# A decode kernel: a second copy of x loaded in 18 one-row pieces on GpSimd's queue and in row groups of 1, 2, 4 and 8 on ScalarE's

## The chip, the cores and the metric

The kernel runs on one core of a Trainium2 chip. The metric is the device time in microseconds of one execution. Each set of runs gives a median; one execution is also recorded by the hardware profiler, and the profile's times count from the start of that execution's span.

## The reference

One decode step: x of 8 rows and 512 columns is normalised, goes through attention over the last 2048 positions of a key and value cache (32 query heads, 8 cache heads of 128), and through a gated unit whose result gates the attention's output.

```python
B, Sq, D = 8, 1, 512                  # Hq, Hkv, Sk, Dh = 32, 8, 8192, 128; F = 1792
xn = layernorm(x)
q = (xn @ wq)                         # to [B, 32, 1, 128]
k = k_cache[:, :, Sk - W:, :]         # W = 2048, each cache head for 4 query heads
v = v_cache[:, :, Sk - W:, :]
p = softmax(q @ k^T * Dh ** -0.5)
s = (p @ v) @ wo
g = silu((sigmoid(xn @ w_gate) * (xn @ w_up)) @ w_down)
out = x + s * g
```

Inputs and output are bf16. The change concerns the x of the last line.

## The kernel before

**Data.** wq, the windows of both caches, the three weights of the gated unit and wo are read once, 81 MB. They go through `ring`, nine tiles of up to 2048 KB, and all their loads are issued by SyncE (`load`, L88). The order is the list `loads` (L138 to L146): two halves of wq, then tiles of k (`k_sb`) and v (`v_sb`) in the order in which they are due, with w_gate, w_up (`wg_sb`, `wu_sb`) and w_down (`wd_sb`) before the end and wo (`wo_sb`, in pieces) last. In SyncE's order the first are wq0, wq1, k0, k1, k2, k3, v0, k4, v1, then k5, v2, k6, v3, k7, v4, k8. `issue_loads` (L164) issues the next ones whose place in the ring was released.

**Order.** The program's order is written by hand (`manual_schedule`): each engine runs its instructions in the order of the source. The loop at L610 goes through slots t. One slot turns a quarter of a k tile on DVE (`k_turn`, L422), multiplies it with q on the PE (`qk`, L435), and, for an earlier batch row, runs the softmax (`soft_max_part`, `soft_exp`, `soft_turn`, `soft_spread`, `soft_mask`) and the product with v (`pv`, L549; ScalarE copies it out at L560). A batch row has SPB = 8 slots. ScalarE's copy `pc_bf` (L495) belongs to `soft_spread`.

**x.** x is loaded twice. `x_bf` (L97, ScalarE's queue) is for the normalisation. `x2_sb` (L181, called x_sb in the profile) is for the sum at the end: 64 partitions, of which 0 to 7 hold columns 0 to 255 of the 8 rows and 32 to 39 hold columns 256 to 511. It is set to zero on GpSimd and then filled by two loads from GpSimd's queue (L184), ahead of all else that GpSimd does: `ident`, the zeros of `qz_sb` (L194), `SumM` (L232 to L254) and `ones` (L264).

**The end.** After the last tile of v, the PE multiplies with w_down and wo (`a_ps`, L662, piece by piece as wo lands); DVE computes `prod` (L673) and `y_bf` (L675), which reads x2_sb; SyncE and ScalarE each issue one half of the output (L677). Then SyncE checks the semaphores of all engines and queues, two at a time, before the engines meet for the last time (L706 in the profile).

**Semaphores of the loads.** The loads of SyncE and ScalarE take turns on eight completion semaphores, HW0 to HW7, those of GpSimd on eight others, SW0 to SW7. A load that takes a semaphore waits, on its issuing engine, until the load that had it before has landed. Before the change, x_bf has HW0, wq0 has HW1, wq1 HW2, k0 to k3 have HW3 to HW6, v0 HW7, k4 HW0, v1 HW1: so v1 waits for wq0, k5 for wq1, v2 for k0.

Of the kernel before, what the change touches and what calls it, by code (L numbers as in the profile page):

```python
# [10 lines left out]
def kernel(  # L11
# [13 lines left out]
    nc = tc.nc  # L25
    P = 128
    B, _, D = A_x.shape
# [23 lines left out]
    SPB = NG * NJ  # L51
# [10 lines left out]
    NCOL = 2  # L62
    DC = D // NCOL
# [29 lines left out]
    def ring_tile(shape, name):  # L93
        return ring.tile(shape, bf16, name=name, tag="ring", align_bytes=ALIGN)
# [7 lines left out]
    for kh in range(2):  # L102
        t = ring_tile([P, KH, Hq * Dh], f"wq_sb{kh}")
# [76 lines left out]
    issue_loads()  # L180
    x2_sb = work.tile([NCOL * 32, DC], bf16, name="x2_sb")  # L181
    nc.gpsimd.memset(x2_sb[:], 0.0)
    for j in range(NCOL):
        nc.gpsimd.dma_start(  # L184
            out=x2_sb[32 * j : 32 * j + B, :],
            in_=A_x.flatten_outer_dims()[:, DC * j : DC * (j + 1)],
        )

    ident = consts.tile([P, P], bf16, name="ident")
    make_identity(nc, ident[:])  # L190
# [18 lines left out]
        out=rstd[:], in_=mv[:, 1:2], func=AF.Sqrt, bias=eps_t[:], scale=1.0  # L209
# [4 lines left out]
        out=xn_bf[:],  # L214
# [7 lines left out]
    for kt in range(KT):  # L222
        nc.tensor.transpose(
            out=xnT_ps[:, kt, :], in_=xn_bf[:B, kt::KT], identity=ident[:B, :B]
# [8 lines left out]
    for off in range(-rep * (NQ - 1), rep * NQ, rep):  # L233
        nc.gpsimd.affine_select(
            out=SumM[:],
            in_=SumM[:],
# [9 lines left out]
        out=SumM_blk,  # L246
        in_=SumM_blk,
# [7 lines left out]
        out=SumM_blk,  # L255
        in_=SumM_blk,
# [5 lines left out]
    )  # L262
    ones = consts.tile([P, P], f32, name="ones")
    nc.gpsimd.memset(ones[:], 1.0)  # L264

    Jneg = consts.tile([P, NQ], f32, name="Jneg")
    nc.vector.tensor_reduce(
        out=Jneg[:],
        in_=ident[:].rearrange("p (a j r) -> p j a r", j=NQ, r=rep),
# [4 lines left out]
        out=Jneg[:], in0=Jneg[:], scalar1=-scale, scalar2=None, op0=ALU.mult  # L274
# [4 lines left out]
        out=Hm[:],  # L279
        in_=ident[:].rearrange("p (a gl) -> p gl a", gl=GL),  # L280
# [5 lines left out]
    for w in (32, 64):  # L286
        Sel[w] = consts.tile([P, w], f32, name=f"Sel{w}")
        nc.vector.tensor_reduce(
            out=Sel[w][:],
            in_=ident[:].rearrange("p (a m) -> p m a", m=w),  # L290
# [7 lines left out]
    for Q in range(NQ):  # L298
        nc.vector.tensor_copy(
            out=spread[:, :, Q, 32 * Q : 32 * (Q + 1)].rearrange(  # L300
                "m c (k g) -> m c g k", g=GL
            ),
            in_=ident[:].rearrange("m (g c k) -> m c g k", c=C4, k=KQ),
# [74 lines left out]
    def q_out(gg, q_ps, on_dve):  # L378
        HW = rep * Dh
        q_sb = ppool.tile([P, HW], bf16, name="q_sb", tag="p_bf")  # L380
        nc.scalar.copy(
            out=q_sb[:].rearrange("p (y e w) -> p y e w", e=2, w=32),
            in_=q_ps[:].rearrange("p (y w e) -> p y e w", e=2, w=32),
        )
        qT_sb = ppool.tile([P, HW], bf16, name="qT_sb", tag="pt_bf")
        nc.vector.transpose(out=qT_sb[:], in_=q_sb[:])  # L386
        for gl in range(GL):
            for Q in range(NQ):
                c0 = rep * NQ * gg + rep * Q
                out = qz_sb[32 * Q : 32 * (Q + 1), :, GL * gg + gl, :, c0 : c0 + rep]  # L390
                in_ = qT_sb[32 * gl : 32 * (gl + 1), :].rearrange(
                    "p (r y b) -> p b y r", r=rep, b=32
                )[:, :B]
                if Q in on_dve:
                    nc.vector.tensor_copy(out=out, in_=in_)  # L395
                else:
                    nc.scalar.copy(out=out, in_=in_)  # L397
# [16 lines left out]
    def k_turn(t):  # L414

        i, j = divmod(t, NJ)
        kw = (
            k_tiles[i][:, CC * j : CC * (j + 1), :]
            .rearrange("p c d -> p (c d)")
            .bitcast(f32)  # L420
        )
        nc.vector.transpose(out=kw, in_=kw)  # L422

    def qk(t):

        i, j = divmod(t, NJ)
        b, gg = divmod(i, NG)
        a, e = divmod(j, 2)
        if gg == 0 and j == 0:
            s_tiles[b] = psum.tile([P, CH * KQ], f32, name="s_ps")  # L430
        kT = k_tiles[i][:].rearrange(
            "p c (a k g e) -> p c a k g e", a=NA, k=KQ, e=2
        )
        for gl in range(GL):
            nc.tensor.matmul(  # L435
                s_tiles[b][32 * gl : 32 * (gl + 1), :],
                lhsT=qz_sb[:, b, GL * gg + gl, j, :],
                rhs=kT[:, :, a, :, gl, e],
                start=(gg == 0 and j == 0),
                stop=(gg == NG - 1 and j == NJ - 1),  # L440
                tile_position=(0, 32 * gl),
                skip_group_check=True,
            )

    def soft_max_part(b):
        mx = small.tile([P, 1], f32, name="mx")
        nc.vector.reduce_max(out=mx[:], in_=s_tiles[b][:], axis=AX.X)  # L447
        mj = small.tile([P, NQ], f32, name="mj")
        nc.vector.tensor_scalar(  # L449
            out=mj[:], in0=Jneg[:], scalar1=mx[:], scalar2=None, op0=ALU.mult  # L450
        )
        return mj

    def soft_exp(b, mj):
        mb_ps = psum1.tile([P, NQ], f32, name="mb_ps", tag="misc")
        nc.tensor.matmul(mb_ps[:], lhsT=SumM[:], rhs=mj[:], start=True, stop=True)  # L456
        nm = small.tile([P, 1], f32, name="nm")
        nc.vector.tensor_reduce(out=nm[:], in_=mb_ps[:], axis=AX.X, op=ALU.min)  # L458
        den128 = small.tile([P, 1], f32, name="den128")
        p_bf = ppool.tile([P, CH * KQ], bf16, name="p_bf")  # L460
        nc.scalar.activation(  # L461
            out=p_bf[:],
            in_=s_tiles.pop(b)[:],
            func=AF.Exp,
            bias=nm[:],
            scale=scale,
            accum_out=den128[:],
        )
        e_tiles[b] = (p_bf, den128)

    def soft_turn(b):

        p_bf = e_tiles[b][0]
        pt_bf = ppool.tile([P, CB, NG, NQ, rep], bf16, name="pt_bf")
        nc.vector.transpose(  # L475
            out=pt_bf[:].rearrange("p c g q r -> p (c g q r)"), in_=p_bf[:]
        )
        pt_tiles[b] = pt_bf
# [22 lines left out]
    def soft_mask(b):  # L501

        pc = pc_tiles.pop(b)[:].rearrange("p y (h n) -> p (y h) n", h=2)
        pT_tiles[b] = ppool.tile([P, CB * NG * 2, GL, 2 * rep], bf16, name="pT_sb")
        for gl in range(GL):
            nc.vector.tensor_scalar(  # L506
                out=pT_tiles[b][:, :, gl, :],
                in0=pc,
                scalar1=Hm[:, gl : gl + 1],
                scalar2=None,  # L510
                op0=ALU.mult,
            )

    def soft_den_part(b):
        den128 = e_tiles.pop(b)[1]
        dh = small.tile([P, Hq], f32, name="dh")
        nc.vector.tensor_scalar(
            out=dh[:].rearrange("p (G g r) -> p G g r", G=NG, g=GL),
            in0=SumM[:].rearrange("p (g G j r) -> p j G g r", g=GL, G=NG, j=NQ)[:, 0],
            scalar1=den128[:],  # L520
            scalar2=None,
            op0=ALU.mult,
        )
        return dh
# [85 lines left out]
    for t in range(NSLOT + PV_LAG):  # L610
        u = t - PV_LAG
        b, ph = (t - QK_LAG) // SPB - 1, (t - QK_LAG) % SPB
        in_b = 0 <= b < B
        if in_b and ph == 3:
            soft_mask(b)
            dh_of[b] = soft_den_part(b)
        if t < NSLOT:
            k_turn(t)
        if t == 1:
            q_out(1, q_tiles[1], (0,))  # L620
        if in_b and ph == 2:
            soft_turn(b)
        if QK_LAG <= t < NSLOT + QK_LAG:
            qk(t - QK_LAG)
        if in_b and ph == 0:
            mj_of[b] = soft_max_part(b)
        if in_b and ph == 1:
            soft_exp(b, mj_of.pop(b))
        if u >= NJ and u % NJ == 0:
            pv_sum(u // NJ - 1)  # L630
        if u >= 0:
            pv(u)
        if in_b and ph == 2:
            soft_spread(b)
        if in_b and ph == 4:
            soft_den(b, dh_of.pop(b))
        if t % NJ == NJ - 1 and QK_LAG <= t < NSLOT + QK_LAG:
            released.add((0, t // NJ - 1))
        if u >= 0 and u % NJ == NJ - 1:
            released.add((1, u // NJ))  # L640
        issue_loads()
        if u == NSLOT - 2 * NJ - 1:
            unit_in(wg_sb[0])
            unit_in(wu_sb[0])
            released |= {(2, 0), (2, 1)}
            issue_loads()
        if u == NSLOT - 2 * NJ:
            unit_mid()
        if u == NSLOT - NJ:
            o_rows(0)  # L650
# [25 lines left out]
    for c in range(NCOL):  # L676
        queues[c].dma_start(  # L677
            out=out.flatten_outer_dims()[:, DC * c : DC * (c + 1)],
            in_=y_bf[32 * c : 32 * c + B, :],
# [31 lines left out]
```

## Time and profile before

| | |
|---|---|
| median of 3 runs | 198.26 us (198.17 to 198.59) |
| the profiled execution | 198.21 us |
| its span | 196.5 us |
| PE busy | 138.2 us (70%) |
| DVE busy | 117.0 us (60%) |
| ScalarE busy | 32.6 us (17%) |
| GpSimd busy | 9.3 us (5%) |
| read from HBM | 81.02 MB, 412 GB/s over the span |

The profile gives stretches of the span with each engine's busy time and number of instructions, the granted PE clock, the busy share of the 16 DMA engines and what they moved:

```profile
0.00:13.00 13.00, 2.19 (x20) 0.96 (x21) 7.18 (x18) 1.58 (x2) 9.35 (x21) 1.00 0.86 345
13.00:43.00 30.00, 15.84 (x82) 3.94 (x81) 23.98 (x36) 12.08 (x26) 0.00 (x0) 0.93 1.01 433
43.00:100.00 57.00, 51.41 (x303) 17.64 (x300) 38.24 (x63) 7.62 (x15) 0.00 (x0) 0.89 1.01 430
...
183.00:193.00 10.00, 8.14 (x94) 6.49 (x92) 1.14 (x2) 0.38 (x1) 0.00 (x0) 0.71 0.91 363
193.00:196.50 3.50, 0.28 (x2) 0.09 (x1) 0.69 (x2) 0.00 (x0) 0.00 (x0) 0.87 0.02 5
```

The columns are the stretch in us, its length, then PE, PE weight load, DVE, ScalarE (ACT) and GpSimd (POOL). GpSimd works in the first stretch alone. Beside these views, the trace has a record of each DMA packet (queue, start, time taken, size) and of each of the 16 completions of a load, one by each DMA engine; it doesn't name the engine. In the profile a name followed by q, as SPq, is an engine's instruction queue.

### The profile page before, as it was taken

The numbers are of one execution on the slowest core, as the hardware profiler recorded it, in microseconds if no ns is written. First come the engines' busy times: TensorE is split into PE (matmuls) and PEld (weight loads), VectorE is DVE, ScalarE is ACT, GpSimd is POOL, SyncE is SP. The second block draws the span as 40 slices with busy tenths as digits, with TensorE's granted clock in tenths as the row PEclk, the third lists the DMA queues.
The fourth block names the chain that finished last, engine by engine and source line by source line (L and its number), as shares of the span: only waits on it lengthen the run. The fifth ranks groups of instructions, "written<-read, shape, count | busy, mean of one in ns | idle before, by whom it ended". The sixth has DMA issues, their size and how long they took to land.

```text
span 196.5 us, 2699 instructions
## 1 busy us (share of the span) xinstructions
PE 138.2 (70%) x1112; PEld 57.6 (29%) x1112; DVE 117.0 (60%) x200; ACT 32.6 (17%) x68; POOL 9.3 (5%) x21
## 2 busy tenths in 40 slices
PE   0340078669998987899789278946794779674783
PEld 0110011032324222423333044404240424443661
DVE  3818999746686828664777277837773750361101
ACT  3008540410121102101210021002100210340000
POOL 8820000000000000000000000000000000000000
PEclk9999999955999997879999957996888587996579
DMA  6999999999999999999999999999999999999991
GB/s 215 429 427 427 430 434 429 440 434 427 434 427 434 427 427 427 430 434 430 430 434 434 424 427 440 430 425 427 430 434 430 427 431 434 423 424 420 411 391 41
DMA packets 6860, 81.19 MB, mean 413 GB/s; under 512 B 792, under 2 KB 1088, under 8 KB 2112
## 3 DMA queue, kind: packets, MB, share of 16 engines
q1 hardware_dynamic: 6752, 81.01, 97.1%
q8 instruction: 8, 0.13, 0.2%
q10 hardware_dynamic: 32, 0.01, 0.1%
q14 instruction: 4, 0.03, 0.0%
q0 software_dynamic: 64, 0.01, 0.0%
HBM read 81.02 MB, written 0.01 MB: 412 GB/s over the span
## 4 chain that ended last, share of the span: by engine, by line
DMA 72%; DVE 17%; PE 8%; ACT 1%; issue 1%; SPq 0%; DVEq 0%; ACTq 0%
DMA k_sb<-in_A_k_cache_dram 47%; DMA wd_sb<-in_B_w_down_dram 14%; DVE k_sb L422 11%; DMA wq_sb<-in_A_wq_dram 6%; DMA wo_sb<-in_A_wo_dram 5%; PE pT_ps L486 3%; PE s_ps L435 3%; DVE qz_sb L395 2%; PE acc_ps L549 1%; DVE mx L447 1%; DVE qT_sb L386 1%; DVE pt_bf L475 1%; ACT L461 1%; PE q_ps L367 1%; PE mb_ps L456 0%
## 5 line engine op out<-in xcount | busy, mean ns | idle before, releaser
L422 DVE STREAM_TRANSPOSE k_sb<-k_sb 128x1024 f32<-128x1024 f32 x64 | 75.9, 1219 | 16.6 <-DMA k_sb<-in_A_k_cache_dram 16.5
L435 PE MATMUL s_ps<-k_sb,qz_sb 128*32 128x512 bf16 x256 | 68.7, 1065 | 16.4 <-DVE k_sb L422 11.6
L549 PE MATMUL acc_ps<-v_sb,pT_sb 128*32 128x256 bf16 (+1 forms) x416 | 35.3, 345 | 3.9 <-DMA v_sb<-in_A_v_cache_dram 2.6
L549 PEld LDWEIGHTS <-pT_sb 128*32 128x32 bf16 (+1 forms) x416 | 12.5, 109 | 33.2 <-issue 27.0
L506 DVE TENSOR_SCALAR pT_sb<-pc_bf,Hm 128x512 bf16<-128x512 bf16 x32 | 9.1, 349 | 18.3 <-ACT pc_bf L495 18.3
L435 PEld LDWEIGHTS <-qz_sb 128*32 128x32 bf16 x256 | 8.3, 100 | 34.0 <-issue 26.1
L560 ACT COPY acc_sb<-acc_ps 128x256 f32<-128x256 f32 (+1 forms) x16 | 7.2, 453 | 63.2 <-PE acc_ps L549 63.2
L486 PE MATMUL pT_ps<-pt_bf,spread 128*128 128x128 bf16 x128 | 12.5, 272 | 6.3 <-DVE pt_bf L475 6.3
L570 PEld LDWEIGHTS oT_ps<-Sel,acc_sb 128*128 128x128 f32 x88 | 11.8, 202 | 14.3 <-ACT acc_sb L560 8.5
L570 PE MATMUL oT_ps<-Sel,acc_sb 128*128 128x16 f32 x88 | 13.4, 276 | 1.1 <-ACT acc_sb L560 1.1
L486 PEld LDWEIGHTS <-spread 128*128 128x128 bf16 x128 | 10.8, 123 | 10.8 <-DVE pt_bf L475 10.8
L456 PE MATMUL mb_ps<-mj,SumM 128*128 128x4 f32 x16 | 3.5, 286 | 14.3 <-DVE mj L449 14.3
L461 ACT ACTIVATE p_bf<-s_ps,nm 128x512 bf16<-128x512 f32 x8 | 5.5, 687 | 46.5 <-DVE nm L458 46.5
L577 DVE TENSOR_TENSOR oT_sb<-oT_ps,rden 128x16 bf16<-128x16 f32 x16 | 2.6, 160 | 11.7 <-PE oT_ps L570 11.7
L456 PEld LDWEIGHTS mb_ps<-mj,SumM 128*128 128x128 f32 x16 | 2.8, 218 | 22.5 <-DVE mj L449 20.6
L397 ACT COPY qz_sb<-qT_sb 32x128 bf16<-32x128 bf16 x20 | 8.3, 413 | 3.0 <-DVE qT_sb L386 2.7
L530 DVE RECIPROCAL rden<-den_ps 128x32 f32<-128x32 f32 x8 | 2.8, 351 | 7.3 <-PE den_ps L528 7.3
L495 ACT CAST pc_bf<-pT_ps 128x512 bf16<-128x512 f32 x8 | 4.7, 587 | 13.1 <-PE pT_ps L486 13.1
L367 PE MATMUL q_ps<-wq_sb,xnT_sb 128*32 128x512 bf16 x32 | 3.8, 625 | 4.0 <-DMA wq_sb<-in_A_wq_dram 4.0
L475 DVE STREAM_TRANSPOSE pt_bf<-p_bf 128x512 bf16<-128x512 bf16 x8 | 5.4, 679 | 1.9 <-ACT p_bf L461 1.9
L662 PE MATMUL a_ps<-wo_sb,o_sb 128*32 128x256 bf16 x64 | 5.5, 315 | 1.0 <-DMA wo_sb<-in_A_wo_dram 0.9
L447 DVE TENSOR_REDUCE mx<-s_ps 128x1 f32<-128x512 f32 x8 | 5.3, 657 | 0.0
(61 smaller groups left out, 61.9 us busy)
## 6 DMA issues: line engine op xcount, KB each, us to landing
k_sb<-in_A_k_cache_dram SPq DMA_DIRECT2D x16, 2048.0 KB, 31.8
v_sb<-in_A_v_cache_dram SPq DMA_DIRECT2D x16, 2048.0 KB, 29.5
wq_sb<-in_A_wq_dram SPq DMA_DIRECT2D x2, 2048.0 KB, 9.7
wo_sb<-in_A_wo_dram SPq DMA_DIRECT2D x2, 1024.0 KB
wg_sb<-in_B_w_gate_dram SPq DMA_DIRECT2D x1, 1792.0 KB, 29.3
wu_sb<-in_B_w_up_dram SPq DMA_DIRECT2D x1, 1792.0 KB, 30.1
wd_sb<-in_B_w_down_dram SPq DMA_DIRECT2D x1, 1792.0 KB, 27.6
wo_sb<-in_A_wo_dram SPq DMA_DIRECT2D x3, 512.0 KB, 23.5
```

The costliest lines, as they stand in the source:

```text
L397: nc.scalar.copy(out=out, in_=in_)
L422: nc.vector.transpose(out=kw, in_=kw)
L435: nc.tensor.matmul(s_tiles[b][32 * gl : 32 * (gl + 1), :], lhsT=qz_sb[:, b, GL * gg + gl, j, :], rhs=kT[:, :, a, :, gl, e], start=(gg == 0 ...
L447: nc.vector.reduce_max(out=mx[:], in_=s_tiles[b][:], axis=AX.X)
L456: nc.tensor.matmul(mb_ps[:], lhsT=SumM[:], rhs=mj[:], start=True, stop=True)
L461: nc.scalar.activation(out=p_bf[:], in_=s_tiles.pop(b)[:], func=AF.Exp, bias=nm[:], scale=scale, accum_out=den128[:],)
L475: nc.vector.transpose(out=pt_bf[:].rearrange("p c g q r -> p (c g q r)"), in_=p_bf[:])
L486: nc.tensor.matmul(pT_ps[:, :, c4, :], lhsT=spread[:, c4, Q, :], rhs=pt[:, :, Q, :], start=(Q == 0), stop=(Q == NQ - 1), skip_group_check= ...
L506: nc.vector.tensor_scalar(out=pT_tiles[b][:, :, gl, :], in0=pc, scalar1=Hm[:, gl : gl + 1], scalar2=None, op0=ALU.mult,)
L549: nc.tensor.matmul(acc_tiles[i][w * c : w * (c + 1), :], lhsT=pT[:, 32 * y : 32 * y + w], rhs=v_tiles[i][:, ch : ch + n_ch, :].rearrange(" ...
L560: nc.scalar.copy(out=acc_sb[:], in_=acc_tiles.pop(i)[:])
L570: nc.tensor.matmul(oT_ps[:], lhsT=acc_sb[:, Dh * c : Dh * (c + 1)], rhs=sel[:, c // 2, c % 2], start=(c == 0), stop=(c == n_ch - 1),)
```

## The change

The two loads of x2_sb are replaced by 23 smaller ones.

- Rows 0 to 7 of the left half (partitions 0 to 7) are loaded one row at a time, row 0 in four pieces and each other row in two: 18 loads of 31, 37, 79, 109, 17, 239, 23, 233, 29, 227, 59, 197, 83, 173, 89, 167, 107 and 149 columns. They are on GpSimd's queue, after `ones`.
- The right half (partitions 32 to 39) is loaded on ScalarE's queue in five loads: the first 17 columns in groups of 1, 2, 4 and 1 rows, and the other 239 columns of all 8 rows. They stand in the loop at slot t = 16, which on ScalarE is after the first `pc_bf` copy and before the first `acc_sb` copy.

```diff
-    for j in range(NCOL):
-        nc.gpsimd.dma_start(
-            out=x2_sb[32 * j : 32 * j + B, :],
-            in_=A_x.flatten_outer_dims()[:, DC * j : DC * (j + 1)],
-        )
+    x_rows = A_x.flatten_outer_dims()
+    CUT = ((31, 68, 147), (17,), (23,), (29,), (59,), (83,), (89,), (107,))
+
+    def load_x2_top():
+        for b in range(B):
+            cuts = (0, *CUT[b], DC)
+            for c0, c1 in zip(cuts, cuts[1:]):
+                nc.gpsimd.dma_start(
+                    out=x2_sb[b : b + 1, c0:c1], in_=x_rows[b : b + 1, c0:c1]
+                )
+
+    def load_x2_low():
+        n = CUT[1][0]
+        for r0, r1, c0, c1 in (
+            (0, 1, 0, n),
+            (1, 3, 0, n),
+            (3, 7, 0, n),
+            (7, 8, 0, n),
+            (0, 8, n, DC),
+        ):
+            nc.scalar.dma_start(
+                out=x2_sb[32 + r0 : 32 + r1, c0:c1],
+                in_=x_rows[r0:r1, DC + c0 : DC + c1],
+            )
...
     ones = consts.tile([P, P], f32, name="ones")
     nc.gpsimd.memset(ones[:], 1.0)
+    load_x2_top()
...
         if t == 1:
             q_out(1, q_tiles[1], (0,))
+        if t == 2 * SPB:
+            load_x2_low()
```

The built program differs in four more places, all of them waits.

- On GpSimd, the ninth of the 18 loads waits for the first, the tenth for the second, and so on, eight semaphores being all there are.
- ScalarE's five loads take HW1 to HW5, after wq0, wq1, k0, k1 and k2. v1 now takes HW6 and waits for k3, k5 takes HW7 and waits for v0, v2 takes HW0 and waits for k4, k6 takes HW1 and waits for ScalarE's first load, v3, k7, v4 and k8 for its second to fifth. From the load after k8 on, each again waits for SyncE's load eight places before it.
- Ahead of y_bf, DVE checks the semaphores of x2_sb's loads in five instructions of two each; it was one.
- At the very end, SyncE's checks are ten where they were seven. Before, the last two of the seven were those of the two output loads' semaphores (with two engines'); now those are the sixth and seventh of ten.

## The prediction

> **What bounds the kernel now.** I read the page first: the DMA row of the slices, the queues, and the shares of the chain that ended last. GpSimd's queue is q0 (software), ScalarE's is q10, SyncE's is q1.
>
> ```profile
> DMA  6999999999999999999999999999999999999991
> ...
> q1 hardware_dynamic: 6752, 81.01, 97.1%
> ...
> q10 hardware_dynamic: 32, 0.01, 0.1%
> ...
> q0 software_dynamic: 64, 0.01, 0.0%
> ...
> DMA 72%; DVE 17%; PE 8%; ACT 1%; issue 1%; SPq 0%; DVEq 0%; ACTq 0%
> ```
>
> The reader is to see that the 16 DMA engines are full from the second slice to the last but one, and that q1, SyncE's stream of weights and caches, is nearly all of it. A 2048 KB load at the 430 GB/s of the middle slices takes 2.097 MB / 430 GB/s = 4.88 us. Loads wait some 30 us in the queue (31.8 us is the median from issue to landing for a k tile), so issuing one a few us later changes nothing so long as another one stands in front of it. The DVE pieces of the chain lie before such a 30 us queue and are covered by it. Next I read the chain in order of time, for its end.
>
> ```profile
> 183.06 9.89 DMA wo_sb<-in_A_wo_dram
> ...
> 192.99 0.30 PE a_ps L662 x2
> ...
> 193.32 0.42 DVE prod L673
> ...
> 193.76 0.28 DVE y_bf L675
> ```
>
> The stream ends at 192.95; two matmuls, two DVE operations and the output DMAs follow, and end the 196.5 us span. So the time is the stream's length plus this tail, and the change costs what it adds to one of them. In the trace's completion records the last piece of wo lands on the first of 16 engines at 191.18 and on the last at 192.95: the slowest engine sets the end.
>
> **The loads taken off the start.** From the timeline of GpSimd:
>
> ```profile
> 1.41 1.17 POOL L184 DMA_DIRECT2D x_sb<-in_A_x_dram  x2 [0.30 <-POOL x_sb L182]
> 2.57 0.23 POOL masks.py:197 MEMSET ident<- 128x128 bf16 x1
> ...
> 10.59 0.36 POOL L264 MEMSET ones<- 128x128 f32 x1
> ```
>
> Without them ident and all that follows on GpSimd start 1.17 us earlier. I cost this at nothing: the PE's projection waits for wq until 13.13, and DVE's copies of q begin at 15.69, long after GpSimd has ended (10.95). Were that cover gone it would be worth 1.17 us at most. The two loads' 64 packets go from q0. In the trace's packet records they are 16 of 512 bytes at 27 ns and 48 of 4 bytes at 9 ns: 864 ns, or 0.05 us on each of 16 engines. That is the gain.
>
> **The 18 loads on GpSimd.** They stand behind ones, so from about 10.95 - 1.17 = 9.8 us. An issue took 0.59 us (1.17 / 2), and landing 6.1 to 6.4 us. The ninth waits for the first and so on: 8 x 0.59 = 4.7 us for a batch, then the wait for the batch's first landing; three batches, the last landing near 30 us. Nothing stands behind them on GpSimd until the end of the kernel, and y_bf needs them at 193.76. What they cost is engine time. One load made 32 packets, 8 of data and 24 of 4 bytes. With one row there is one of data; I take 31 of 4 bytes: 31 x 9 + about 20 = 0.30 us, 18.7 ns on each engine, 18 times 0.34 us. Upper bound: as dear as the 8-row load (432 ns, 27 ns an engine), 0.49 us. Lower bound: one of data and one completion an engine, 16 x 9 + 20 = 164 ns, 10.2 ns an engine, 0.18 us. Does it add to the stream? Between 5.5 and 8.0 us, where q0's packets ran, q1's share in the records fell from 16.1 to 15.85 engines, that is 0.04 us an engine for the 0.05 us of q0: yes. Net of the 0.05 removed: +0.29 us (0.13 to 0.44).
>
> The Trainium skill, "DMA: Bandwidth & Descriptors", section "Measured", speaks against the change: a GpSimd load has a floor of 64 packets at about 10.5 ns, 0.67 us. The trace has 32 packets and 0.43 us a load. By the page the 18 loads would make 18 x 0.67 / 16 = 0.75 us an estimate, and the forecast 0.4 us more.
>
> **The five loads on ScalarE.** From the timelines of ScalarE and SyncE:
>
> ```profile
> 42.06 0.59 ACT L495 CAST pc_bf<-pT_ps 128x512 bf16<-128x512 f32 x1 [2.72 <-PE pT_ps L486]
> 51.02 0.59 ACT L560 COPY acc_sb<-acc_ps 128x512 f32<-128x512 f32 x1 [8.38 <-PE acc_ps L549]
> ```
> ```profile
> 8.47 0.54 SPq L91 DMA_DIRECT2D v_sb<-in_A_v_cache_dram  x1
> 13.20 0.53 SPq L91 DMA_DIRECT2D k_sb<-in_A_k_cache_dram  x1
> 18.04 0.53 SPq L91 DMA_DIRECT2D v_sb<-in_A_v_cache_dram  x1
> 28.93 0.54 SPq L91 DMA_DIRECT2D k_sb<-in_A_k_cache_dram  x1
> ```
>
> They are issued between these two ScalarE rows, from 42.65. An issue on ScalarE took 0.31 (output) to 0.60 us (x_bf): 1.6 to 3.0 us, inside the 8.38 us that ScalarE idles. Their own semaphore waits (the first five loads of SyncE, landed by 27.7) are over by then.
>
> Packets: on q10 an 8-row load has 8 of data and 8 of 4 bytes. So 1, 2, 4, 1 and 8 rows make 32 packets. Spread over 16 engines they cost 0.05 us; all on one row's engine, five of data (27 to 46 ns in the output's records, say 36) and five of 9 ns, 0.22 us; and nothing, if that engine is one that ends early. I take 0.10 us (0 to 0.22).
>
> **SyncE's issues.** By the changed program's waits, v1 (issued at 8.47) waits for k3, k5 (13.20) for v0, v2 (18.04) for k4, and k6 (28.93) for the first of ScalarE's loads. In the completion records k3, v0 and k4 have landed on all engines at 33.28, 38.13 and 42.97. At each of these times two whole loads, 9.8 us of work, still stand in the queue, so no engine runs dry. k6 can go when ScalarE's first load lands: 42.65 + 0.6, and 1.2 us (x_bf's landing on an empty queue, 1.41 to 2.6) to 6.4 us (x_sb's), so 44.5 to 49.7. Before it stand v1, k5 and v2, the last of which ends at 56.45. A gap opens only if that load lands after some 54 us. I cost it at nothing; this cover is 4 to 10 us. Queued behind k6 on SyncE are v3, k7 and the rest; the rows of before issue k7 at 43.10 and v4 at 51.02, so they are late by at most those few us, under the same cover.
>
> **The tail.** y_bf's semaphore checks on DVE go from one instruction to five:
>
> ```profile
> L675 DVEq EVENT_SEMAPHORE  x1: 49/49/49, 193.3 to 193.3; - x1
> ```
> ```profile
> L706 SPq EVENT_SEMAPHORE  x9: 17/28/28, 194.9 to 196.4; - x9
> ```
>
> Five of 49 ns are 0.25 us, under prod's 0.42; if prod did not cover them, +0.2 us. At the end SyncE goes through all semaphores, one check each 69 ns (they start at 194.98, 195.05, 195.12, 195.19 in the trace). Before, the two for the output DMAs came last, at 195.37 and 195.55. Now three stand behind them: +3 x 0.069 = +0.21 us (0 to 0.21).
>
> **Sum.** +0.29 + 0.10 + 0.21 = +0.60 us on the profiled execution's 198.21 us (196.5 span and 1.71 around it): 198.81. The median of the runs is 198.26, 0.05 above that execution; I stay with 198.8. With the terms' own bounds (0.13 to 1.07 with the DVE checks) 198.35 to 199.3.
>
> **The rivals.** *The small packets are free* (0.18). The windows show a DMA share of 1.01, more than 16 engines busy, so an engine has two packets under way and a 9 ns one may slip beside a 611 ns one. Then the stream ends where it did and only the end checks are left: 198.21 + 0.21 = 198.42, no change (within 0.2%). It decides if the last wo lands at 192.95 as before. Against it: the fall of q1's share by 0.25 engine.
>
> *A small packet of ScalarE's is dearer than its record* (0.14). The 16 KB instruction packets of q8 took 0.93 us by their records, yet the engine that had one lags by 1.4 us afterwards (completions of one load at 71.0 and at 72.7): 0.43 us that no record holds, with the 8 KB ones of q14 the same (0.31 recorded, 0.75 lag). Five such on one engine are 2.2 us. If it is one that ends early (1.5 us before the last), 0.7 of it shows: 198.21 + 0.29 + 0.21 + 0.7 = 199.4; else 200.9. The Trainium skill, "DMA: Bandwidth & Descriptors", section "Why a DMA increments its semaphore by 16 and not by 1", would put them on one engine: such a transfer takes the lowest-numbered engines. No view here names the engines.
>
> *SyncE starves* (0.04): ScalarE's first load lands after 54 us; each us beyond costs one. At 57 us: 201.8. Only a lateness of DVE's first stage by 4 us or more, by GpSimd's loads beside it, could do it: x_sb's loads of before ran while DVE idled, so no row shows that price, but DVE's L213 beside the 3.51 us GpSimd memset took 2.40 us.
>
> **How the numbers follow.** The sum has 0.58, the rivals 0.18, 0.14 and 0.04; 0.06 are left for a gain, for which no step is at hand but the lag between engines coming out otherwise (1.77 us between first and last). About 0.2%, 0.4 us, is what a measurement of this kernel can tell from no change: slower is above 198.66. Of the sum's 0.58 I give 0.50 to that side. Slower: 0.50 + 0.14 + 0.04 = 0.68; same: 0.08 + 0.18 = 0.26; faster: 0.06. The range is 198.35 (end checks and the lower bound of the packets) to 199.9 (half of the second rival); out of it lie the gain, half of that rival and the third, 0.17.
>
> **What would show it.** q0 with some 576 packets (306 at the lower bound), q10 with 64; the last wo landing at 193.2 to 193.4; no idle DMA between 33 and 60 us, though v1, k5, v2 and k6 are issued at about 33, 38, 43 and 45 to 50; y_bf 0.02 us behind prod; 0.2 us more between the outputs' landing and the end. Wrong would make it: packets by the element (thousands on q0), one engine far behind the others, a DMA digit under 9, or DVE standing between prod and y_bf.

## The result, and the profile after

| | before | after |
|---|---|---|
| median of 11 runs each, side by side | 198.35 us (198.0 to 199.26) | 198.93 us (198.75 to 199.7) |
| the profiled execution | 198.21 us | 198.91 us |
| its span | 196.5 us | 196.8 us |
| the execution less its span | 1.71 us | 2.11 us |
| last piece of wo landed | 192.95 us | 193.09 us |
| span, mean over executions | 196.46 us (98) | 196.81 us (19) |
| time less span, median over executions | 1.76 us (98) | 2.11 us (19) |

The last two rows take every execution for which a span is on record, those of the experiments' sets and of the two repeats among them. One execution of the kernel before, of 223.5 us, was in a slower state and is left out.

The ratio is 1.0031 with a 95% interval of 1.0018 to 1.0044: slower, by about 0.6 us. The forecast was 198.8 us and its likeliest case was slower, so the number came out. The table already shows that its working did not come out: only half of the lost time lies in the span (0.30 of the profiled executions' 0.70 us; 0.35 of 0.70 us over all executions), and the prediction put all of it there.

The page of after, its slices, queues and shares of the chain (the columns of a queue are packets, MB, share of 16 engines):

```profile
DMA  5999999999999999999999999999999999999991
...
q1 hardware_dynamic: 6752, 81.01, 96.9%
...
q0 software_dynamic: 576, 0.01, 0.2%
...
q10 hardware_dynamic: 64, 0.02, 0.0%
...
DMA 72%; DVE 16%; PE 7%; ACT 1%; issue 1%; SPq 0%; ACTq 0%; DVEq 0%
```

q0 has 576 packets for 18 loads, 32 each, and q10 has 32 more, both as forecast. q1 carries the same 6752 packets in a share 0.2 points lower, because the same work takes a span 0.3 us longer. No slice between the second and the last but one lost its 9.

GpSimd's timeline of after (start, time of the group, what, and in brackets what it waited for):

```profile
1.04 0.20 POOL masks.py:197 MEMSET ident<- 128x128 bf16 x1
...
8.76 0.20 POOL L284 MEMSET ones<- 128x128 f32 x1
8.91 4.67 POOL L190 DMA_DIRECT2D x_sb<-in_A_x_dram  x8
15.00 0.52 POOL L190 DMA_DIRECT2D x_sb<-in_A_x_dram  x1 [1.43 <-DMA x_sb<-in_A_x_dram]
...
24.84 0.52 POOL L190 DMA_DIRECT2D x_sb<-in_A_x_dram  x1 [0.72 <-DMA x_sb<-in_A_x_dram]
```

ident is at 1.04 where it was at 2.57. Eight loads go out in 4.67 us, and each of the next waits for one eight places earlier; the last is issued at 24.84 and landed near 34 us. y_bf reads them 160 us later. So all this waiting costs nothing by itself; what can cost is the packets.

ScalarE and SyncE in after, from their timelines:

```profile
41.91 1.45 ACTq L203 DMA_DIRECT2D x_sb<-in_A_x_dram  x5
50.83 0.59 ACT L581 COPY acc_sb<-acc_ps 128x512 f32<-128x512 f32 x1 [8.34 <-PE acc_ps L570]
```
```profile
33.62 0.54 SPq L91 DMA_DIRECT2D v_sb<-in_A_v_cache_dram  x1
38.31 0.53 SPq L91 DMA_DIRECT2D k_sb<-in_A_k_cache_dram  x1
43.10 0.54 SPq L91 DMA_DIRECT2D v_sb<-in_A_v_cache_dram  x1
46.63 0.54 SPq L91 DMA_DIRECT2D k_sb<-in_A_k_cache_dram  x1
```

The five issues ran beside the pc_bf copy (the forecast had them behind it) and end long before acc_sb. SyncE's v1, k5 and v2 went out 25 us later than before (v1 at 33.62 for 8.47) and k6 17.7 us later (46.63 for 28.93), at the forecast places. The windows of after, with DMA share and GB/s as the last two columns, show that the DMA engines stayed full:

```profile
42.00:52.00 10.00, 8.96 (x40) 1.92 (x37) 7.27 (x11) 1.08 (x2) 0.00 (x0) 0.69 0.99 423
52.00:100.00 48.00, 42.39 (x258) 15.09 (x257) 30.34 (x49) 7.02 (x14) 0.00 (x0) 0.93 1.01 431
```

The kernel before has 424 and 431 GB/s in the same two stretches. The end of after's chain of waits (start, length, what):

```profile
183.14 9.95 DMA wo_sb<-in_A_wo_dram
...
193.13 0.30 PE a_ps L685 x2
...
193.46 0.06 DVE prod L696
193.52 0.05 issue
193.57 0.05 DVEq L698
193.62 0.05 issue
193.66 0.05 DVEq L698
...
193.86 0.05 DVEq L698
193.91 0.04 issue
193.95 0.28 DVE y_bf L698
```

The stream still sets the end. New are the DVEq entries: y_bf's five semaphore checks, of 0.05 us with 0.05 between one and the next, run beside prod (193.46 to 193.87) and outlast it. By the records y_bf starts 0.085 us behind prod's end; before, it was 0.035. At the very end SyncE's row has three checks more:

```profile
L729 SPq EVENT_SEMAPHORE  x12: 17/28/28, 194.7 to 196.7; - x12
```

In its records the check of the second output starts at 195.74, the three that follow it at 195.80, 195.86 and 195.92, and the drain behind them at 195.99. Before, the drain came 0.07 us behind that check; now it comes 0.25 us behind.

**How far the stream is late.** A whole-kernel median can't split 0.3 us of stream into parts, but the packet records can: sort q1's large packets by the time they end, and subtract from each the time of the packet of the same rank in the kernel before. The table has the mean over 64 packets, in us, at three places of the stream, for after and for the experiments told below. A constant offset is mostly the start's jitter (0.05 to 0.14); what grows is what the change costs the stream. For the two loads that were moved, whose packets begin at 12.6 us, the first column is the mean between 8.5 and 12 us.

| | at 13 us | at 37 us | at 62 us | growth | q0's recorded time between, on each of 16 engines |
|---|---|---|---|---|---|
| after | -0.14 | +0.08 | +0.10 | 0.24 | 0.33 |
| after, again | -0.08 | +0.14 | +0.16 | 0.24 | 0.33 |
| 18 GpSimd loads alone | -0.08 | +0.14 | +0.14 | 0.22 | 0.33 |
| 36 GpSimd loads | -0.13 | +0.52 | +0.78 | 0.91 | 0.65 |
| 8 GpSimd loads | -0.09 | +0.02 | +0.02 | 0.11 | 0.16 |
| 5 ScalarE loads alone | -0.08 | -0.08 | -0.06 | 0.02 | 0 |
| 8 ScalarE loads | -0.10 | -0.10 | +2.13 | 2.23 | 0 |
| two loads, moved | -0.08 | -0.04 | -0.04 | 0.04 | 0.05 |
| no loads | -0.05 | -0.05 | -0.05 | 0.00 | 0 |
| before, again | -0.14 | -0.14 | -0.14 | 0.00 | 0 |

After loses its 0.22 us between 13 and 37 us, where GpSimd's packets run (12.6 to 33.5 us), 0.02 more where ScalarE's are, and nothing later.

The table begins behind the place of the two loads taken off the start (5.6 to 7.9 us). The same comparison between the stretches 3.5 to 5.3 and 8.5 to 12 us has their price: programs with neither of the two loads there gain 0.02 to 0.04 us on the kernel before, those with one of them 0.02, and those that keep both (before again, and the six copies told below) stay within 0.002.

The growth is a mean over all DMA engines, but the kernel's end waits for the slowest. The last piece of wo landed at 193.07 to 193.29 us in the five profiles with the 18 GpSimd loads, 193.14 in the mean, and at 192.81 to 193.05 us in six with at most two GpSimd loads (before, before again, five ScalarE loads, two loads moved, no loads, six copies), 192.96 in the mean. That is 0.18 us later, with 0.2 us between single profiles of each group.

### The profile page after: what moved, and what is told of

It reads as the page before. It is cut to its first block, busy times and chain, and to the rows that moved or that the text cites. A ratio compares the mean times of both kernels' runs of the same rounds, so it can differ in the third digit from the quotient of the medians.

```text
span 196.8 us, 2730 instructions
## 1 busy us (share of the span) xinstructions
PE 140.4 (71%) x1112; PEld 58.6 (30%) x1112; DVE 117.2 (60%) x200; ACT 32.5 (17%) x68; POOL 17.5 (9%) x37
## 3 DMA queue, kind: packets, MB, share of 16 engines
q1 hardware_dynamic: 6752, 81.01, 96.9%
## 4 chain that ended last, share of the span: by engine, by line
DMA 72%; DVE 16%; PE 7%; ACT 1%; issue 1%; SPq 0%; ACTq 0%; DVEq 0%
DMA k_sb<-in_A_k_cache_dram 44%; DMA wd_sb<-in_B_w_down_dram 14%; DVE k_sb L443 11%; DMA wq_sb<-in_A_wq_dram 6%; DMA wo_sb<-in_A_wo_dram 5%; DMA x_sb<-in_A_x_dram 3%; PE pT_ps L507 3%; PE s_ps L456 2%; DVE qz_sb L416 2%; PE acc_ps L570 1%; DVE mx L468 1%; DVE pt_bf L496 1%; DVE qT_sb L407 1%; ACT L482 1%; PE q_ps L388 1%
## 5 line engine op out<-in xcount | busy, mean ns | idle before, releaser
L456 PE MATMUL s_ps<-k_sb,qz_sb 128*32 128x512 bf16 x256 | 68.0, 1060 | 16.0 <-DVE k_sb L443 11.6
L570 PE MATMUL acc_ps<-v_sb,pT_sb 128*32 128x256 bf16 (+1 forms) x416 | 36.0, 355 | 1.9 <-DVE pT_sb L527 1.0
L507 PE MATMUL pT_ps<-pt_bf,spread 128*128 128x128 bf16 x128 | 13.3, 282 | 6.3 <-DVE pt_bf L496 6.3
L591 PEld LDWEIGHTS oT_ps<-Sel,acc_sb 128*128 128x128 f32 x88 | 12.3, 210 | 14.9 <-ACT acc_sb L581 8.9
L591 PE MATMUL oT_ps<-Sel,acc_sb 128*128 128x16 f32 x88 | 13.9, 282 | 1.2 <-DVE rden L551 0.7
L507 PEld LDWEIGHTS <-spread 128*128 128x128 bf16 x128 | 11.4, 128 | 11.1 <-DVE pt_bf L496 11.1
L190 POOL DMA_DIRECT2D x_sb<-in_A_x_dram x18 | 9.9, 554 | 6.5 <-DMA x_sb<-in_A_x_dram 6.5
```

The source lines that it names most:

```text
L190: nc.gpsimd.dma_start(out=x2_sb[b : b + 1, c0:c1], in_=x_rows[b : b + 1, c0:c1])
L456: nc.tensor.matmul(s_tiles[b][32 * gl : 32 * (gl + 1), :], lhsT=qz_sb[:, b, GL * gg + gl, j, :], rhs=kT[:, :, a, :, gl, e], start=(gg == 0 ...
L507: nc.tensor.matmul(pT_ps[:, :, c4, :], lhsT=spread[:, c4, Q, :], rhs=pt[:, :, Q, :], start=(Q == 0), stop=(Q == NQ - 1), skip_group_check= ...
L570: nc.tensor.matmul(acc_tiles[i][w * c : w * (c + 1), :], lhsT=pT[:, 32 * y : 32 * y + w], rhs=v_tiles[i][:, ch : ch + n_ch, :].rearrange(" ...
L591: nc.tensor.matmul(oT_ps[:], lhsT=acc_sb[:, Dh * c : Dh * (c + 1)], rhs=sel[:, c // 2, c % 2], start=(c == 0), stop=(c == n_ch - 1),)
```

## The experiments

Each edit is against the kernel before unless it says otherwise. Ratios are to the kernel before of the same set of runs, with a 95% interval.

**The 18 GpSimd loads alone.** The right half goes in one GpSimd load at the start.

```diff
-    for j in range(NCOL):
-        ...
+    nc.gpsimd.dma_start(out=x2_sb[32:32 + B, :], in_=x_rows[:, DC:2 * DC])
...
     nc.gpsimd.memset(ones[:], 1.0)
+    load_x2_top()
```

> Only the 18 GpSimd pieces; the right half stays one GpSimd load at the start. Theory S (the sum: packets, checks): q0 has 18 x 32 + 32 = 608 packets, 0.35 us an engine. The output DMAs' semaphores are the last checked again, so the 0.18 us of end checks is gone; DVE has four checks before y_bf, 98 ns apart (0.39 us), just under prod's 0.41. Span 196.5 + 0.2 to 0.35. Theory O (time outside the span grows with the number of GpSimd loads: 1.71 us with 2, 2.11 with 18): time less span 2.1 us, in all 198.25 + 0.6 to 0.75. If the time outside is chance, it is alike in all four kernels of this call and the total is +0.2 to 0.35.

198.74 us, ratio 1.0022 (1.0004 to 1.0041), span 196.6. The end of its chain:

```profile
193.46 0.42 DVE prod L684
193.88 0.02 issue
193.91 0.28 DVE y_bf L686
```

With one half in one load y_bf has four checks, which end inside prod: no DVEq entry is left, and y_bf starts 0.03 behind prod. The outputs' checks are the last two again, with the drain 0.06 us behind. So the two tail terms of after are gone here, and what remains in the span is the stream: 0.22 us of growth. The median is 0.48 us above the 198.26 of the kernel before in this set, though, and the spans only 0.2 (196.6 against 196.4 in the median). The rest lies outside the span: 2.04 us in the median of its 12 executions, against 1.76. So theory O's time was met; the 36 loads below speak against its reason.

**The five ScalarE loads alone.** The left half goes in one GpSimd load at the start.

```diff
-    for j in range(NCOL):
-        ...
+    nc.gpsimd.dma_start(out=x2_sb[0:B, :], in_=x_rows[:, 0:DC])
...
+        if t == 2 * SPB:
+            load_x2_low()
```

> Only ScalarE's five loads, with SyncE's changed waits; the left half stays one GpSimd load at the start. Theory S: 32 more packets on q10, 0.05 us of stream; the output DMAs' semaphores are second and third of six, three checks behind them, +0.18 us; the gain of one load less at the start up to 0.08 us. Span 196.5 + 0.1 to 0.25. v1 issued at 33 to 34 us and no idle DMA. Theory O: one GpSimd load, time less span 1.7 us; total +0.1 to 0.25. Rival (the later issues of v1, k5, v2 and k6 cost something): the last wo lands 0.3 us or more later than at 192.95.

198.39 us, ratio 0.9994 (0.9981 to 1.0007), span 196.5 in the profile and 196.6 in the median of 12 executions, 0.2 above the kernel before of this set; 1.73 us outside the span in the median. The end checks are as in after (0.25 us from the second output's check to the drain), v1 is issued at 33.17, and the stream grows by 0.02 us. The price of these loads' packets is nearly nothing, and a late v1, k5, v2 and k6 cost nothing under the cover that the prediction named.

**The two whole loads behind `ones`.**

```diff
-    for j in range(NCOL):
-        nc.gpsimd.dma_start(out=x2_sb[32*j : 32*j+B, :], ...)
...
     nc.gpsimd.memset(ones[:], 1.0)
+    for j in range(NCOL):
+        nc.gpsimd.dma_start(out=x2_sb[32*j : 32*j+B, :], ...)
```

> The two whole loads moved behind ones, nothing else. Theory S with a start that gains: the first load, wq0, lands 0.35 us earlier (as in the changed kernel: 7.69 to 8.11 against 8.05 to 8.45), and the later loads give 0.05 us back; span 196.5 - 0.15 to + 0.05. Rival (the start gains nothing): wq0 lands early but the load after it does not, span 196.5. Theory O: two GpSimd loads, time less span 1.7 us.

198.39 us, ratio 1.0 (0.9981 to 1.0019), span 196.5. GpSimd's earlier start is worth nothing that shows.

**No loads: ScalarE copies x_bf.**

```diff
-    for j in range(NCOL):
-        nc.gpsimd.dma_start(out=x2_sb[32*j : 32*j+B, :], ...)
...
+    for j in range(NCOL):
+        nc.scalar.copy(out=x2_sb[32*j : 32*j+B, :], in_=x_bf[:, DC*j : DC*(j+1)])
     q_tiles = q_projection()
```

> No loads of x2_sb: ScalarE copies both halves out of x_bf ahead of the projection, in its idle time before 14.25 us. Theory S: q0 empty, one check fewer on DVE (hidden behind prod), one fewer on SyncE; span 196.5 - 0.2 to 0. Theory O: no GpSimd load, time less span 1.65 us or less, total -0.25 to 0. If the time outside the span depends on the GpSimd queue being in use at all, it falls by more here than between 2 and 18 loads.

198.12 us, ratio 0.9992 (0.9975 to 1.001), span 196.4; q0 is empty. This is the most that could be had from x2_sb's loads, and it can't be told from the kernel before. The best form of this step is to not load x a second time, but it gains nothing that can be measured.

**36 GpSimd loads.** Every piece of the 18 is cut in two; otherwise as in the first experiment.

```diff
             cuts = (0, *CUT[b], DC)
+            cuts = sorted({*cuts, *(c + 7 + b for c in cuts[:-1])})
```

> Each of the 18 GpSimd pieces cut in two; the right half one GpSimd load at the start. The checks are those of the kernel with 18 pieces (four on DVE, ten at the end, outputs last). Theory S (packets): 37 x 32 = 1184 packets, 0.68 us an engine, 0.33 more than with 18 pieces: last wo 0.3 us later than there (193.1). Theory O (time outside the span grows with the loads on GpSimd, 0.025 us each): time less span 2.6 to 2.8 us where 18 pieces had 2.1 to 2.4. Together +0.7 to 0.8 us on the 198.74 of 18 pieces: 199.4 to 199.6. If the time outside depends on the eight GpSimd semaphores in use, it stays at 2.1 to 2.4 and the total is 199.0 to 199.1.

199.33 us, ratio 1.0057 (1.0033 to 1.008), span 197.3, q0 1184 packets. The stream grows by 0.91 us, but not evenly: 0.45 of it comes between 17.8 and 21.5 us, where only about three of the 36 loads run. It begins with a quarter of a microsecond in which the records have only 13.1 engines busy, and packets of 16 KB take up to 872 ns there (the median is 611). The other 0.46 us are 14 ns for each of the other 33 loads, where the 18 loads had 0.22 / 18 = 12 ns. The slow stretch was seen in the one profile that there is, and its cause stays open. But the spans of all ten executions are 197.1 to 197.6 us, 1.0 us above those of the kernel before in the mean, so a loss of about this size is in each of them, and the cost isn't proportional to the number of loads. The time outside the span was 1.71 us (1.79 in the median), so that time doesn't grow with the number of GpSimd's loads.

**Eight GpSimd loads of two rows, behind `ones`.** All eight of GpSimd's semaphores are used once.

```diff
     nc.gpsimd.memset(ones[:], 1.0)
+    for j in range(NCOL):
+        for r in range(0, B, 2):
+            nc.gpsimd.dma_start(out=x2_sb[32*j+r : 32*j+r+2, :], ...)
```

> Eight loads of two rows on GpSimd behind ones, none at the start: all eight GpSimd semaphores in use, the same checks as with 18 pieces. Theory S: 256 packets, 0.15 us an engine; last wo near 193.0, y_bf 0.03 to 0.04 us behind prod. Theory O by the number of loads: time less span 1.85 us, total 198.26 + 0.1 to 0.3. If the time outside goes by the semaphores in use: time less span 2.1 to 2.4 as with 18 pieces, total 198.26 + 0.4 to 0.6.

198.12 us, ratio 1.0001 (0.9983 to 1.0019), span 196.6, q0 256 packets. Growth 0.11 us for 8 loads, 14 ns each: with two rows of data a load still makes 32 packets and costs what a one-row piece costs. The number of semaphores in use costs nothing that shows: the profiled execution had 2.47 us outside its span, but the median of the 12 is 1.72.

**Eight ScalarE loads.** As the five, but the right half in one load a row; then k5, not k6, is the first to wait for ScalarE.

```diff
     def load_x2_low():
-        for r0, r1, c0, c1 in ((0, 1, 0, n), (1, 3, 0, n), (3, 7, 0, n), (7, 8, 0, n), (0, 8, n, DC)):
+        for r0, r1, c0, c1 in [(r, r + 1, 0, DC) for r in range(B)]:
```

> The right half in eight one-row loads on ScalarE; the left half one GpSimd load at the start. By the waits of this program v1 waits for k3 and k5 for ScalarE's second load, so k5 can go at about 46.5 us, when v1 is the only load in front of it and ends at 46.8 to 48.5. Theory S (the cover is the work in the queue): the first engines run dry for up to 1 us between 46.8 and 47.7, the late ones do not; last wo 0 to 0.9 us later. Rival (the later issues cost nothing at all): DMA share 1.00 or more in that stretch, last wo within 0.1 us of 192.95.

200.77 us, ratio 1.012 (1.0093 to 1.0147), span 198.7. SyncE's timeline, its waits (total, times, longest in us) and the windows:

```profile
33.25 0.54 SPq L91 DMA_DIRECT2D v_sb<-in_A_v_cache_dram  x1
47.01 0.53 SPq L91 DMA_DIRECT2D k_sb<-in_A_k_cache_dram  x1
```
```profile
SPq L91 <- DMA x_sb<-in_A_x_dram: 13.1, 1, 13.1
```
```profile
45.00:46.00 1.00, 0.98 (x4) 0.10 (x3) 1.00 (x1) 0.00 (x0) 0.00 (x0) 1.00 1.07 459
46.00:47.00 1.00, 1.00 (x14) 0.50 (x10) 0.09 (x1) 0.00 (x0) 0.00 (x0) 1.00 0.25 102
47.00:48.00 1.00, 1.00 (x7) 0.15 (x8) 0.95 (x2) 0.00 (x0) 0.00 (x0) 1.00 0.04 16
48.00:49.00 1.00, 1.00 (x8) 0.14 (x8) 1.00 (x2) 0.00 (x0) 0.00 (x0) 1.00 0.82 262
```

SyncE sat 13.1 us in one wait for a load of ScalarE. Behind v1 nothing stood in the queue, the DMA share fell from 1.07 to 0.25 and 0.04, and the stream lost 2.2 us that the rest of the kernel never gave back. This is the prediction's third rival, which the change as made escapes: there, k6 is the waiting load, issued at 46.63 with the end of v1 and all of k5 and v2 ahead of it. The expected size was too small: most engines had finished v1 between 46.3 and 46.8 us, and the records have k5's first packets at 48.34, 1.3 us after SyncE began the issue at 47.01. The 16 GB/s of the stretch before 48 are the last packets of v1.

**The kernel before, again.** The unchanged program.

> The kernel before, unchanged: what two looks at one program differ by. Last wo within 0.1 us of 192.95, span 196.5 within 0.1; time less span 1.7 us if that number is the program's own (theory O), up to 2.1 or more if it is chance.

198.33 us, ratio 1.0017 (0.9998 to 1.0036); span 196.4, and 198.87 for the profiled execution, 2.45 us more than its span. So the time outside the span differs by 0.74 us between two executions of one program, and a difference between two profiled executions alone proves little. The medians over many executions, told further down, are what can be compared.

**The changed kernel, again.**

> The changed kernel, unchanged, beside the three below. Theory S (packets, checks): the stream is late by 0.2 us between 12 and 50 us and by nothing more later; y_bf 0.08 us behind prod; 0.25 us from the second output's check to the first drain. Total 198.2 + 0.6. Theory I (ScalarE's five added instructions move a fetch of its instructions from the end of the span to 184 us, and the next one falls behind the span's end): time less span 2.1 us again.

198.98 us, ratio 1.0033 (1.0022 to 1.0044), span 196.8, profiled 198.88 (2.08 outside). Against the repeated kernel before, the last wo lands 0.12 us later, y_bf stands 0.05 us farther behind prod and the drain 0.18 us farther behind the outputs' check: 0.35 us, as much as the two spans differ by.

**y_bf reads a copy.** Against the changed kernel: GpSimd copies x2_sb at slot 32, so that y_bf doesn't wait for the loads.

```diff
+        if t == 4 * SPB:
+            nc.gpsimd.tensor_copy(out=x3_sb[:], in_=x2_sb[:])
...
-    nc.vector.tensor_tensor(out=y_bf[:], in0=prod[:], in1=x2_sb[:], op=ALU.add)
+    nc.vector.tensor_tensor(out=y_bf[:], in0=prod[:], in1=x3_sb[:], op=ALU.add)
```

> The changed kernel, with y_bf reading a copy of x2_sb that GpSimd makes at slot 32, long after all loads have landed. Theory S: one check on DVE ahead of y_bf, which follows prod by 0.02 us instead of 0.08; the end checks stay (three behind the outputs', 0.25 us). Span 0.06 us below the changed kernel's, total within 0.1 us of it. If the checks cost more than the trace of one execution shows, the total falls by 0.2 us or more.

199.07 us, ratio 1.0039 (1.0023 to 1.0055), span 196.9. Its chain:

```profile
193.52 0.42 DVE prod L699
193.94 0.03 issue
193.97 0.02 DVEq L701
193.99 0.04 issue
194.03 0.28 DVE y_bf L701
```

The five checks are gone, and y_bf is again 0.10 us behind prod by the records: the one check left starts after prod's end. The expected 0.02 was missed. The copy replaces one small wait by another, and moves no packet.

**Six small copies on ScalarE.** A test of whether ScalarE's number of instructions moves the time outside the span.

```diff
+        if t == 2 * SPB:
+            for _ in range(6):
+                nc.scalar.copy(out=idle_sb[:], in_=ones[:, 0:1])
```

> The kernel before with six copies of one column on ScalarE at slot 16, in its idle time (five instructions more in all, as many as the five loads are). Theory I: the 8 KB instruction packet that before came at 195.5 us comes at about 184, and time less span goes from 1.71 to 2.0 or 2.1: total 198.2 + 0.3. Theory S alone: no packet, no check added, total as before within 0.1 us.

198.25 us, ratio 1.0002 (0.9991 to 1.0012), span 196.5, 1.71 outside (1.80 in the median): no effect. The instruction packet stayed near the end, at 195.9 us, so the move that theory I needs did not come about.

**Four such copies, in the changed kernel**, behind its ScalarE loads.

```diff
             load_x2_low()
+            for _ in range(4):
+                nc.scalar.copy(out=idle_sb[:], in_=ones[:, 0:1])
```

> The changed kernel with four such copies on ScalarE behind its five loads, which makes as many ScalarE instructions as the kernel with eight ScalarE loads has (there the packet came at the end again and time less span was 1.71). Theory I: time less span 1.7 us, total 0.3 to 0.4 us below the changed kernel's. Theory S alone: total as the changed kernel within 0.1 us.

199.08 us, ratio 1.0046 (1.003 to 1.0062), 2.09 outside the span (2.12 in the median): no effect on it either, and the packet stayed at 184.3 us. The count of ScalarE's instructions is not what lengthens it. About the place of the packet these two runs say nothing, since it did not move.

## Why the prediction was right, and where it was not

**Direction and total: right, and the total in good part by luck.** +0.60 forecast, +0.58 by the medians, and both kinds of cost that it named, packets in a full stream and checks at the end, are in the trace. But the terms that it named come to 0.44 us as measured (0.22 and 0.02 of packets, less the 0.03 gained at the start, 0.05 of y_bf's checks and 0.18 of end checks), and with the engines' last meeting 0.08 shorter 0.36 are left. The spans of all executions differ by 0.35. The rest came from a place where the prediction had put no change, the time outside the span.

**GpSimd's packets: count right, price too high.** 32 a load, 576 in all, 0.33 us of recorded time on each engine, as the base case had it. The stream lost 0.22 us: 12 ns a load on each engine, not the 18.7 taken. That is near the lower bound of 10.2, but in the number alone, since that bound had half the packets. The rows of 8 and 36 loads give 14 ns each (without the slow stretch). So a third of the recorded time did not add to the stream, and the "yes" of the prediction was too strong: its own figure, 0.04 us of q1 lost for 0.05 of q0, already had less than all of it. The first rival, that small packets slip in beside large ones, would account for that third, but no view shows the packets of one engine, so how it happens is not shown. The Trainium skill, "DMA: Bandwidth & Descriptors", section "Measured", whose loads cover 128 partitions, would have 64 packets and an estimate of 0.75 us for the 18 loads. The trace has half the packets in these loads of one partition, and less than a third of the time on the stream.

**The two loads taken off the start: 0.05 us forecast as gain, 0.02 to 0.04 measured.** Moving them behind `ones` gave the same 0.04 back. GpSimd's 1.17 us (1.53 in the trace) were hidden, as said.

**ScalarE's five loads: 0.10 forecast, 0.02 measured.** The second rival, 2.2 us on one engine, fell with that: in the run of the five loads alone the last piece of wo landed at 192.81 on its slowest engine, not later than before.

**SyncE's later issues: free, as said, and for the reason given.** The eight loads show the price when nothing is left in the queue as the wait ends: 2.2 us.

**y_bf's checks: mis-sized.** The prediction took five checks as 5 x 49 = 0.25 us under prod. They start 97 ns apart, so the last ends 0.44 us after the first starts, past prod's 0.41: +0.05 us. y_bf was not "0.02 us behind prod".

**The end checks: +0.21 forecast, +0.18 measured,** three of 60 ns.

**The forecast place of the last wo, 193.2 to 193.4, was missed** (193.09; 193.07 in the repeat): the packet terms were too large.

**The lower end of the range was worked out wrongly.** The prediction calls 198.35 "end checks and the lower bound of the packets", but 0.21 and 0.13 us on 198.21 are 198.55; 198.35 is the packets' lower bound alone.

**What no step had: 0.35 us outside the span.** 0.14 of wo, 0.05 of y_bf and 0.18 of end checks are 0.37, and the profiled spans differ by 0.30 (0.08 went with the shorter last meeting). The profiled executions differ by 0.70. The span of each execution is on record to 0.1 us, so the time outside can be compared over many executions:

| | executions | time outside, median | lowest |
|---|---|---|---|
| before, and before again | 98 | 1.76 | 1.67 |
| after, and after again | 19 | 2.11 | 2.06 |
| after, y_bf reads a copy | 6 | 2.09 | 2.03 |
| after, four copies on ScalarE | 10 | 2.12 | 2.06 |
| 18 GpSimd loads alone | 12 | 2.04 | 1.96 |
| 36 GpSimd loads | 10 | 1.79 | 1.67 |
| 8 GpSimd loads | 12 | 1.72 | 1.67 |
| 5 ScalarE loads alone | 12 | 1.73 | 1.68 |
| 8 ScalarE loads | 5 | 1.73 | 1.67 |
| two loads, moved | 12 | 1.76 | 1.68 |
| no loads | 12 | 1.77 | 1.67 |
| six copies on ScalarE | 12 | 1.80 | 1.72 |

The four programs with the 18 GpSimd loads have 2.04 to 2.12 us, all others 1.72 to 1.80. Single profiled executions hide this: the five ScalarE loads had 1.99 in theirs, the kernel before 1.71 and once 2.45. Two things that look like a cause are ruled out by the two halves of the change. The five ScalarE loads alone have three end checks behind the outputs', and one 8 KB instruction packet of q14 at 183.8 us in place of the end, as the changed kernel has; but their time outside is that of before. The 18 GpSimd loads alone have neither (the packet is at 195.7 us), and their time outside is long. A count of GpSimd loads, of semaphores or of ScalarE's instructions is ruled out by the runs with 36 loads, 8 loads and the small copies. So the extra 0.3 us or more comes with the 18 loads, but by what step stays open: the trace has no instruction of the program outside the span.

## What to carry to other kernels

On a stream that filled all DMA engines, small loads on another queue cost engine time by their number of packets (32 a load for one row or two), at two thirds to four fifths of what their packets' records add up to; but 36 loads cost more than twice what 18 did, so a price for one load is no safe rule. Compare packets of the same rank between two traces before believing either. Where queues share completion semaphores in turn, adding loads to one queue makes another queue's loads wait for them: count how many whole loads still stand ahead when the wait ends, since with two it was free and with none it cost 2.2 us. A sum that comes out can hide wrong terms; split the measured difference by the landing of the last load, the tail and the time outside the span before calling its steps right, and take the last of these from many executions.

## What had not been expected of the hardware

- A GpSimd load made 32 packets whether it moved one row, two or eight; the stream lost 12 to 14 ns for each load of one or two rows on each engine, where the records add up to 18.5 (0.333 us / 18) and 20 (0.162 us / 8).
- DVE's semaphore checks last 49 ns but start 97 ns apart.
- With the queue dry, the first packets of a load flowed 1.3 us after SyncE began its issue (47.01 and 48.34).
- The time of an execution outside its span was 1.71 or 2.45 us for the same program; its median over many executions was 1.72 to 1.80 us for most programs and 2.04 to 2.12 us for those with the 18 GpSimd loads.
- With 36 GpSimd loads the stream lost 0.45 us between 17.8 and 21.5 us in the one profile, and the spans of ten executions were 1.0 us longer in the mean. The cause is open.
